# A gated mix of softmax attention and a feature-map attention on one core: one level of a sum tree changes its engine, and the last four output tiles are put together in another way

## The chip, the core and the metric

The kernel runs on one core of a Trainium2 chip. The core has five engines that work side by side: TensorE (PE in the profile, its weight loads PEld), VectorE (DVE), ScalarE (ACT), GpSimd (POOL) and SyncE (SP), which issues most DMA transfers. The metric is the device time of one execution in microseconds; before the change its median over three runs is 758.91 (758.51 to 759.47).

## The reference

`x` has 2048 tokens of 512 values. Branch A is softmax attention with 32 heads of 16 values. Branch B maps queries and keys with a small matrix per head, takes softmax of the result and of its negative, and uses these as features of a linear attention. A sigmoid gate mixes the two.

```
q, k, v = split(x @ A_wqkv)                       # 32 heads of 16
a = softmax(q k^T / 4) v  @ A_wo
q, k, v = split(x @ B_wqkv)
phi(u) = concat(softmax(u w_phi), softmax(-u w_phi))
b = (phi(q) (phi(k)^T v)) / (phi(q) sum(phi(k)) + 1e-6)  @ B_wo
g = sigmoid(sum(x * gate_w))
out = g * a + (1 - g) * b                          # 2048 x 512, bfloat16
```

## The kernel before, in words

**Units.** The scores of branch A are cut into units of 128 keys by 512 queries of one head. Four units make a pack (`p`), 16 packs a group (four heads against all keys for one chunk of 512 queries), and 32 groups the whole: 512 packs (`NPACK`), 2048 units. TensorE writes the scores of a unit to a PSUM bank (`_scores`, L1028). Most units go in pairs to ScalarE, which takes the exponential of 128x1024 values in one instruction (`_exp`, L1076). Four of the eight PSUM banks are a ring for these pairs (`NRING`); the other four are lent out in the order of the plan for everything else.

**Tiles of VectorE.** 500 units go to VectorE instead, which approximates the exponential in integer arithmetic: one instruction per unit from PSUM (L935), and for each batch of four units two further steps in SBUF (L960). `NUMS` gives how many units of each of the 32 groups go this way, and `_plan_vector` spreads them over the group's packs; `REND` (in the last group) and `REST` say how many packs at the group's end stay free. The value matmuls (L1135) add both kinds to one accumulator per group. When a group is done, VectorE transposes the accumulator (L1156), multiplies by the gate and the inverse of the denominator (L1164, L1171, L1173), and the result goes to `onTA`, in the last group by another transpose (L1187).

**Branch B.** `_b_pair` works on two token tiles of 128 at a time. It projects (L706), copies to SBUF (L1294), negates on GpSimd (L1312), takes a maximum tree on VectorE (L1315, L1317), subtracts (L1320), takes the exponential on ScalarE (L1323, 128x2048), and then sums over 16 features by a tree: the first level, 1024 sums, on VectorE (L1325), the levels of 512 and 256 (L1327) and of 128 (L1330) on GpSimd. `P_SUM` sets which levels go to GpSimd: a level of n features goes there when n is at most `P_SUM`, and the first one when `P_SUM` is over 4. An approximate reciprocal on GpSimd follows (`_reciprocal`, L1380 to L1386). There are 16 such pairs, eight for keys and eight for queries. GpSimd also masks the queries of the next two groups (L798) and multiplies in the normalisation (L1173 in all but the last two groups).

**Outputs.** Each of the 16 token tiles of the output is one PSUM bank: four matmuls with `WoB` (`_b_out`, named `outb`), four with `WoA` (in `_out`, named `outa`, all L706), then one drain to bfloat16 and one store. The last four, tiles 12 to 15, make the tail: their fourth `outa` matmul needs the very last group. Tiles 12 and 14 are drained by VectorE (L1612) and stored from SyncE's queue, tiles 13 and 15 by ScalarE (L1609) and stored from ScalarE's queue (L1614). `FIRST_OUT` and `NEXT_OUT` say how many packs before the end the first two and the last two of them may begin; `DEP_OUT` tells which of them wait only for the last VectorE tiles (`last_bits`) and which for the last value matmul (`pvs[-1]`).

**The order of the work.** A planner (`Plan.order`) holds a list of operations with costs, due times (`prio`, counted in packs) and dependences, simulates the engines and writes out a fixed order for each of them. `port` in it keeps GpSimd's work and some of VectorE's from being planned at the same time. `Plan.shift` moves every due time that is not negative by a pseudo-random amount of at most three packs; `SEEDS` has one seed for each 16 packs. Each engine then runs its list in order and waits on semaphores.

Of the kernel before, what the change touches and what calls it, by code (L numbers as in the profile page):

```python
# [7 lines left out]
ALU = mybir.AluOpType  # L8
# [3 lines left out]
D = 512  # L12
H = 32
DH = 16
TOK = 128
QCH = 512
SCALE = float(DH) ** -0.5
F32, BF16 = dt.float32, dt.bfloat16
# [47 lines left out]
class Plan:  # L66
# [43 lines left out]
    def op(self, eng, fn, cost, reads=(), writes=(), deps=(), name="", prio=0.0, rel=-99, kind="full",  # L110
           acquire=None, release=None, lat=None, array=None, strips=None, also=None):
        o = Op(eng, fn, cost, name, prio, rel, kind, self.LAT[eng] if lat is None else lat)
        found = {}
        for b in reads:
            for w in b.writers:
                found[id(w)] = w
        for b in writes:
            for w in b.readers or b.writers:
                found[id(w)] = w
            if b.readers:  # L120
                for w in b.writers:
                    found[id(w)] = w
        for d in deps:
            if d is not None:
                found[id(d)] = d
        found.pop(id(o), None)
        o.deps = list(found.values())
        for b in reads:
            b.readers.append(o)
        for b in writes:  # L130
            b.writers, b.readers = [o], []
        o.acquire, o.release, o.also = acquire, release, also
        o.strips = strips
        o.port = eng == "POOL" or eng == "DVE" and name in self.PORT
        o.held = eng == "PE" and acquire is None and name in self.HOLDING
        o.array = cost if array is None else array
        self.ops.append(o)
        return o

    SEEDS = (3340, 2114, 9789, 849, 7476, 9797, 2928, 4117, 3297, 4434, 5571, 2308, 3491, 3547, 0, 2037, 1043, 5479, 6702, 2263, 0, 95, 4494, 8165, 7230, 4451, 7158, 3400, 9901, 9455, 1584, 0, 4360, 0)  # L140

    def shift(self):
        count = {}
# [264 lines left out]
class _Kernel:  # L408
# [9 lines left out]
    URGENT, AHEAD, SOON, REST = 4, -(1 << 30), 4, 6  # L418
    QDUE, KDUE, VDUE = 20, 17, 14
    P_Q, P_MUL, P_NEG = 1, 1, 1  # L420
    P_REC, P_SUM = 0, 4
    P_BACK, RATIO, BV = 1, 1, 8
    DEN, KV2, P_MAX = 1, 0, 0
    REND = 5
    PAIRQ = 1
    P_M, P_BMUL, CHUNKS = 0, 0, 2
    GDUE = 26
# [1 line left out]
    FAST = 3  # L429
    VSOON = -2  # L430
    PADK = 2
    LAST, FIRST_OUT, NEXT_OUT, DEP_OUT = 0, 8, 0, 2
    ALONE, EARLY = 12, 10
    PVP = 10

# [442 lines left out]
                prio=100))  # L878
        self.b_gB.writers = done

    NUMS = (6, 10, 16, 14, 14, 16, 16, 19, 13, 19, 17, 12, 17, 11, 19, 19, 14, 20, 12, 16, 19, 13, 17, 16, 15, 20, 12, 20, 17, 16, 22, 13)

    def _plan_vector(self):

        NT, away = self.NT, []
        for g in range(self.NPACK // NT):
            n = self.NUMS[g]
            rest = self.REND if g == self.NPACK // NT - 1 else self.REST
            away += [4 * (NT * g + 1 + (2 * k + 1) * (NT - rest) // (2 * n)) + (len(away) + k) % 4 for k in range(n)]
        batches = [away[k:k + self.PACK] for k in range(0, len(away), self.PACK)]  # L890
        self.hooks = {}
        for k, units in enumerate(batches):
            due = max(units[0] / 4 - self.LEAD, self.VMIN)
            self.hooks.setdefault(max(0, int(due) - 4), []).append(
                lambda k=k, units=units, due=due: self._vector_batch(k, units, due))
        for n in range(1, 4 * self.NQC):
            self.hooks.setdefault(max(0, 32 * n - 30), []).insert(0, lambda n=n: self._proj_q(n))
        self.away = set(away)
# [83 lines left out]
    def _attention(self):  # L982
        plan, NT, NQC = self.plan, self.NT, self.NQC
        NU = 4 * self.NPACK
        self.exps, self.qks, self.pvs = [], [], []
        self._plan_vector()
        self.mine = [u for u in range(NU) if u not in self.away]
        self.place = {u: a for a, u in enumerate(self.mine)}
        self.late, self.opened, self.closed, self.in_group = {}, {}, {}, {}
        self.ot = {}  # L990
        self.stores = []
        self.b_outt = [Buf() for _ in range(6)]
        for b in self.b_outt[:2]:
            b.readers = list(self.b_WB.readers)
        self.b_va, self.b_vb = [Buf() for _ in range(self.NA)], [Buf() for _ in range(self.NA)]
        self.b_vs = [Buf() for _ in range(self.NST)]
        self.n_step = 0
        self.last_twin = []
        first = sum(self.GROUPS)
        assert self.mine[first - 1] < 8  # L1000
        for half in range(2):
            a = 0
            for n in self.GROUPS:
                self._qk(a, a + n, half)
                self._exp(a, a + n, half)
                a += n
        while a < len(self.mine):
            b = min(a + self.GROUPS[len(self.exps) % 2], len(self.mine))
            self._qk(a, b)
            self._exp(a, b)  # L1010
            a = b
            done = self.mine[a] if a < len(self.mine) else NU
            while len(self.pvs) < done // 4:
                self._pv(len(self.pvs))
                if len(self.pvs) in self.done:
                    self._out(self.done.index(len(self.pvs)))
# [545 lines left out]

    def _b_out(self, tt):

        job = Job()

        ops = []
        for pr in range(4):
            ops.append(self.plan.op("PE", lambda e, pr=pr: self._wide(
                e, self._bank(job), self.onTB[:, pr, tt * TOK:tt * TOK + TOK], self.WoB[:, pr, :], pr == 0, False),  # L1570
                self.c_pe(512), reads=[self.b_onTB[tt], self.b_WoB], deps=ops[-1:], name="outb",
                acquire=None if pr else job, **self._wide_kind()))
        self.outs.append((job, ops))

    def _out_tile(self, t):
        if t < self.NT - 4:
            return self.outt[:, t % 2, :]
        k = t - self.NT + 4
        return self.xT[:, k, 0:D]

    def _out(self, qc):
        op, NT, NQC = self.plan.op, self.NT, self.NQC
        for tt in range(4):
            t = 4 * qc + tt
            final = qc == NQC - 1
            due = max(self.done[qc] + 8 + 4 * tt, self._num_due(t) + 8)
            job, first = self.outs[t]
            b_onTA = self.b_onTA[qc % 3]
            if final:
                due = self.NPACK  # L1590
                deps = (self.last_bits if tt < self.DEP_OUT else [self.pvs[-1]]) + [w for b in b_onTA[:3] for w in b.writers]
            else:
                deps = [w for b in b_onTA for w in b.writers]
            for x in first:
                x.prio, x.rel = due, due - (6 if not final else self.FIRST_OUT if tt < 2 else self.NEXT_OUT)
                x.deps += deps
            if final:
                due += self.LAST
                for x in first:
                    x.prio = due  # L1600
            m = first[-1]
            for pr in range(4):
                m = op("PE", lambda e, pr=pr, qc=qc, tt=tt, job=job: self._wide(
                    e, self._bank(job), self.onTA[:, qc % 3, pr, tt * TOK:tt * TOK + TOK], self.WoA[:, pr, :], False,
                    pr == 3), self.c_pe(512), reads=[b_onTA[pr], self.b_WoA], deps=[m], name="outa",
                    prio=due + (pr == 3), **self._wide_kind())
            b_outt = self.b_outt[t % 2 if t < NT - 4 else t - NT + 6]
            if final and tt % 2:
                op("ACT", lambda e, t=t, job=job: e.activation(self._out_tile(t), self._bank(job), ACT.Copy),  # L1609
                   self.c_act(512), writes=[b_outt], deps=[m], name="out_ev", prio=due, release=job)  # L1610
            else:
                op("DVE", lambda e, t=t, job=job: e.tensor_copy(self._out_tile(t), self._bank(job)), self.c_dve(512),  # L1612
                   writes=[b_outt], deps=[m], name="out_ev", prio=due, release=job)
            s = self.dma("ACT" if final and tt % 2 else "SP", f"out{t}", lambda e, t=t: e.dma_start(  # L1614
                self.out2d[t * TOK:(t + 1) * TOK, :], self._out_tile(t)), cost=0.36, reads=[b_outt], prio=due)
            self.stores.append(s)
# [43 lines left out]
```

## Time and profile before

| What | us |
|---|---|
| median of three runs | 758.91 |
| the profiled execution | 758.1 |
| its span, first to last instruction | 756.1 |
| ScalarE busy / VectorE busy / GpSimd busy | 742.4 / 717.3 / 210.2 |
| exponentials of branch A on ScalarE (776) | 714.6 |
| end of the last exponential | 748.42 |
| end of the last projection matmul | 753.10 |
| end of the last drain | 753.82 |
| landing of the last store | 755.57 |

Rows of the profile read `line engine operation output<-input shapes xcount | busy us, mean ns of one | idle time before, by whom it ended`. In lists in order of time the first two numbers are the start and the length in us, and square brackets hold idle time and what ended it. Successive instructions of an engine overlap a little at their ends, so the step from one start to the next (0.60 us for a VectorE instruction shown with 0.69, 0.917 for an exponential shown with 1.16) is what one of them displaces. Matmul ends are modelled.

### The profile page before, as it was taken

To read this page: it belongs to the slowest core of one execution; us is meant where nothing else is said; L and a number is where in the kernel's file an instruction comes from. 1 tells how busy PE (TensorE), PEld (TensorE's weight loads), DVE (VectorE), ACT (ScalarE), POOL (GpSimd) and SP (SyncE) were. 2 spreads that over 40 slices of the span, in tenths; PEclk is the share of its full clock that TensorE was granted. 3 is DMA by queue.
4 is the path that set the end of the run, shared out by engine and by line. 5 is a ranking of instruction groups with operands and counts; after the bars stand their busy time and mean duration, and the time that the engine had idled before them with its cause. 6 is when DMAs were issued, how large, how long until landed. Compare 5 with 4: busy or idle time off the path is not lost.

```text
span 756.1 us, 17157 instructions
## 1 busy us (share of the span) xinstructions
PE 745.0 (99%) x7234; PEld 220.1 (29%) x7234; DVE 717.3 (95%) x1128; ACT 742.4 (98%) x798; POOL 210.2 (28%) x301
## 2 busy tenths in 40 slices
PE   8999999999999999999999999999999999999998
PEld 3323322322332222222222322222232223232222
DVE  5788999999999999999999999999999999999994
ACT  6999999999999999999999999999999999999996
POOL 2213205131534334134206051512324050330000
PEclk9999999999999999999999999999999999999999
DMA  9610001000001000000200212211121102111010
GB/s 216 147 25 6 9 8 15 2 3 14 2 2 15 1 8 10 6 11 3 42 15 19 54 23 34 38 27 39 16 43 29 29 22 42 24 33 26 3 15 28
DMA packets 89180, 20.78 MB, mean 27 GB/s; under 512 B 83472, under 2 KB 88592, under 8 KB 89104
## 3 DMA queue, kind: packets, MB, share of 16 engines
q1 hardware_dynamic: 87232, 18.92, 13.2%
q8 instruction: 56, 0.92, 0.5%
q10 hardware_dynamic: 1872, 0.79, 0.5%
q14 instruction: 20, 0.16, 0.1%
HBM read 4.21 MB, written 2.10 MB: 8 GB/s over the span
## 4 chain that ended last, share of the span: by engine, by line
ACT 74%; PE 17%; DVE 7%; DMA 1%; issue 0%
ACT ET L1076 71%; PE ps L1135 7%; PE ps L1028 6%; ACT bq L1323 3%; DVE vs L935 3%; PE ps L706 3%; DVE vs L960 2%; PE ps L1142 1%; DMA xT<-in_A_x_dram 1%; DVE onB L1488 0%; DVE bq L1320 0%; DVE btree L1317 0%; DVE T L1156 0%; DVE btree L1315 0%; PE ps L714 0%
## 5 line engine op out<-in xcount | busy, mean ns | idle before, releaser
L1076 ACT ACTIVATE ET<-ps 128x1024 bf16<-128x1024 f32 (+1 forms) x776 | 714.6, 1155 | 1.7 <-PE ps L1028 1.5
L935 DVE TENSOR_SCALAR vs<-ps 128x512 uint16<-128x512 f32 x500 | 322.6, 684 | 10.7 <-PE ps L1028 8.9
L1028 PE MATMUL ps<-qT,kT 32*128 32x512 bf16 (+1 forms) x2052 | 307.3, 384 | 4.7 <-ACT ET L1076 2.3
L960 DVE TENSOR_SCALAR vs<-vs 128x2048 uint16<-128x2048 uint16 (+1 forms) x250 | 240.3, 972 | 1.3 <-PE ps L1135 0.5
L1135 PE MATMUL ps<-vs,V 128*32 128x512 bf16 x2000 | 211.8, 384 | 0.9 <-DVE vs L960 0.7
L1135 PE MATMUL ps<-ET,V 128*32 128x512 bf16 x1548 | 190.4, 387 | 0.0
L1028 PEld LDWEIGHTS ps<-qT,kT 32*128 32x128 bf16 x2052 | 76.6, 91 | 298.7 <-ACT ET L1076 286.5
L1327 POOL TENSOR_TENSOR btree<-btree 128x512 f16<-128x512 f16 (+1 forms) x32 | 38.5, 1202 | 212.7 <-DVE btree L1325 211.5
L1135 PEld LDWEIGHTS ps<-ET,V 128*32 128x32 bf16 x1548 | 47.9, 94 | 77.9 <-issue 70.7
L1135 PEld LDWEIGHTS ps<-vs,V 128*32 128x32 bf16 x2000 | 48.8, 95 | 55.3 <-issue 33.3
L1142 PE MATMUL ps<-kT,zero 128*32 128x512 bf16 x604 | 61.1, 385 | 0.0
L706 PE MATMUL ps<-WB,xT 128*128 128x512 bf16 x192 | 58.6, 384 | 0.1
L1312 POOL TENSOR_SCALAR bq<-bq 128x1024 bf16<-128x1024 bf16 x16 | 19.1, 1193 | 116.9 <-DVE bq L1294 74.0
L1173 POOL TENSOR_TENSOR T<-T,rinv 128x512 bf16<-128x512 f32 x15 | 18.8, 1252 | 76.9 <-DVE rinv L1171 76.8
L798 POOL TENSOR_SCALAR qT<-qtmp,mask 128x512 bf16<-128x512 bf16 x30 | 29.9, 1001 | 33.0 <-DVE qtmp L793 32.8
L706 PE MATMUL ps<-xT,WA 128*128 128x512 bf16 x120 | 38.1, 384 | 0.1
L1323 ACT ACTIVATE bq<-bq 128x2048 bf16<-128x2048 bf16 x16 | 32.7, 2042 | 0.0
L1156 DVE STREAM_TRANSPOSE T<-ps 128x512 f32<-128x512 f32 x32 | 22.7, 709 | 9.9 <-PE ps L1135 9.9
L1294 DVE CAST bq<-ps 128x512 bf16<-128x512 f32 x32 | 21.8, 685 | 0.1
L839 POOL TENSOR_SCALAR V<-V 128x544 bf16<-128x544 bf16 x16 | 11.5, 721 | 35.8 <-DVE V L832 35.7
L706 PEld LDWEIGHTS ps<-WB,xT 128*128 128x128 bf16 x192 | 13.3, 97 | 25.1 <-issue 20.1
L706 PE MATMUL ps<-WoA,onTA 128*128 128x512 bf16 x64 | 19.8, 383 | 0.0
(89 smaller groups left out, 404.6 us busy)
## 6 DMA issues: line engine op xcount, KB each, us to landing
T<-T SPq DMA_DIRECT2D x240, 8.0 KB, 1.8
WB<-in_B_wqkv_dram SPq DMA_DIRECT2D x1, 1536.0 KB, 8.7
out_dram<-WB SPq DMA_DIRECT2D x12, 128.0 KB, 1.7
WA<-in_A_wqkv_dram SPq DMA_DIRECT2D x2, 384.0 KB, 5.1
WoB<-in_B_wo_dram SPq DMA_DIRECT2D x1, 512.0 KB, 3.9
WoA<-in_A_wo_dram SPq DMA_DIRECT2D x1, 512.0 KB, 4.9
WA<-in_A_wqkv_dram ACTq DMA_DIRECT2D x2, 128.0 KB, 3.3
WA<-in_A_wqkv_dram ACTq DMA_DIRECT2D x1, 256.0 KB, 4.6
```

Of the source, the lines that this page charges most:

```text
L706: return e.matmul(out, lhs, rhs, start=start, stop=stop)
L798: x = self.plan.op("POOL", lambda e, side=side: e.tensor_scalar(self.qT[:, s0 + side, :], tmp, self.mask[:, side:side + 1], 0.0, op0=ALU.m ...
L935: bits = lambda e, to, src: e.tensor_scalar(to, src, SCALE * LOG2E * 128.0, float(ORIGIN), op0=ALU.mult, op1=ALU.add)
L960: o = op("DVE", lambda e, k=k, src=src, dst=dst: e.tensor_scalar(dst, src, float(STEPS[k - 1]), None, op0=ALU.add), 0.16 + k * n * QCH * 0 ...
L1028: return e.matmul(out[:, cols], self.kT[32 * i:32 * i + 32, cp, kt * TOK:(kt + 1) * TOK], self.qT[32 * i:32 * i + 32, s, cols], start=True ...
L1076: o = plan.op("ACT", lambda e: e.activation(self.ET[:, a % NS:a % NS + n, cols], self.ps[:, a % NR:a % NR + n, cols], ACT.Exp, scale=SCALE ...
L1135: ins = e.matmul(self._bank(ot)[32 * i:32 * i + 32, :], v[:, v0:v0 + 32], tile, start=(kt == 0), stop=(kt == self.NT - 1), tile_position=( ...
L1142: ins = e.matmul(self._bank(ot)[32 * i:32 * i + 32, :], self.zero[:], self.kT[:, 0, 0:QCH], start=False, stop=False, tile_position=(0, 32 ...
L1156: t1 = op("DVE", lambda e: e.transpose(T1[:, side].rearrange("p b s -> p (b s)"), src()), 0.735, deps=last, writes=[b_T1[side]], name="n_t ...
L1294: [lambda e, b, k=k: e.tensor_copy(bq[:, k].rearrange("p (g s v) -> p g s v", g=8, s=2)[:, :, 0, :], b.rearrange("p (g v) -> p g v", g=8))],
L1323: op("ACT", lambda e: e.activation(flat, flat, ACT.Exp), 1.789, reads=[b], writes=[b], name="b_exp", prio=due + 1)
L1327: + [("b_sum", two(128 * n), lambda e, n=n: e.tensor_tensor(half[:, :, 0:n], half[:, :, 0:n], half[:, :, n:2 * n], ALU.add), (n <= self.P_ ...
```

## The change

It has four parts.

1. `P_SUM` goes from 4 to 8: the first level of the sum tree, 16 instructions of 128x1024, goes from VectorE to GpSimd.
2. For output tiles 12 and 14 (`_apart`) the four `outb` matmuls form a closed group of their own, due about 20 packs before the end. VectorE copies their result as float32 to a free part of `xT`. The four `outa` matmuls are then a fresh group in another bank, and VectorE's drain becomes an add of that bank and the copy.
3. Tile 15 (`RINGOUT`) takes its bank from the ring, that of the next-to-last pair of units; its matmuls wait for that pair's exponential instead of the last value matmul.
4. Constants: `FIRST_OUT` 8 to 3, `REND` 5 to 4, one tile of VectorE moved from the 16th to the 17th group and one from the 31st to the 30th, and other seeds. The number of VectorE's tiles stays 500. `CUT` and `XT` at the values given change nothing in the batches.

```diff
-    SEEDS = (3340, 2114, 9789, 849, 7476, 9797, 2928, 4117, ...)
+    SEEDS = (0, 825, 9504, 2137, 0, 1384, 1546, 5125, ...)
...
-    P_REC, P_SUM = 0, 4
+    P_REC, P_SUM = 0, 8
...
-    REND = 5
+    REND = 4
+    CUT = 4
+    XT = 0
+    XR = 2
+    RINGOUT = 1
+    APART, APART_AT = 2, 20
...
-    LAST, FIRST_OUT, NEXT_OUT, DEP_OUT = 0, 8, 0, 2
+    LAST, FIRST_OUT, NEXT_OUT, DEP_OUT = 0, 3, 0, 2
...
-    NUMS = (..., 11, 19, 19, 14, 20, ..., 17, 16, 22, 13)
+    NUMS = (..., 11, 19, 18, 15, 20, ..., 17, 17, 21, 13)
...
+    def _apart(self, t):
+        return t >= self.NT - 4 and (t - self.NT + 4) % 2 == 0 and (t - self.NT + 4) // 2 < self.APART
...
             if final:
                 due = self.NPACK
-                deps = (self.last_bits if tt < self.DEP_OUT else [self.pvs[-1]]) + [w for b in b_onTA[:3] for w in b.writers]
+                ring = tt >= 4 - self.RINGOUT
+                deps = self.exps[-2:-1] if ring else self.last_bits if tt < self.DEP_OUT else [self.pvs[-1]]
+                deps = deps + [w for b in b_onTA[:3] for w in b.writers]
...
+            if final and ring and not self._apart(t):
+                first[0].acquire = None
+            apart = self._apart(t)
+            if apart:
+                part, b_part = self.xT[:, tt, 2 * D:4 * D].bitcast(F32), Buf()
+                for x in first:
+                    x.prio, x.rel = due - self.APART_AT + 2 * tt, due - self.APART_AT - 4
+                ev = op("DVE", lambda e, job=job, part=part: e.tensor_copy(part, self._bank(job)), self.c_dve(512),
+                        writes=[b_part], deps=[first[-1]] + [r for b in self.b_xT for r in b.readers], name="outb_ev",
+                        prio=due - self.APART_AT + 2 * tt, release=job)
+                job, first = Job(), []
+            if final and ring:
+                job.bank = (self.bank2[1] + tt - 4 + self.RINGOUT) % self.NRING
...
+            elif apart:
+                op("DVE", lambda e, t=t, job=job, part=part: e.tensor_tensor(self._out_tile(t), self._bank(job), part,
+                                                                             ALU.add), self.c_dve(512), reads=[b_part],
+                   writes=[b_outt], deps=[m], name="out_ev", prio=due, release=None if ring else job)
```

## The prediction

> **What bounds the kernel now.** I read four views in this order: the busy time of each engine, the waits of ScalarE, ScalarE's instructions in order of time, and the last eleven microseconds engine by engine.
>
> Engine totals and the costliest group, from the profile's page:
> ```profile
> PE 745.0 (99%) x7234; PEld 220.1 (29%) x7234; DVE 717.3 (95%) x1128; ACT 742.4 (98%) x798; POOL 210.2 (28%) x301
> ...
> L1076 ACT ACTIVATE ET<-ps 128x1024 bf16<-128x1024 f32 (+1 forms) x776 | 714.6, 1155 | 1.7 <-PE ps L1028 1.5
> ```
> Three engines look full; the waits and ScalarE's own sequence tell which one sets the time.
> ```profile
> ACT xT L1609 <- PE ps L706: 3.6, 1, 3.6
> ...
> ACT ET L1076 <- PE ps L1028: 1.5, 3, 0.7
> ```
> ```profile
> 7.96 2.16 ACT L1076 ACTIVATE ET<-ps 128x512 bf16<-128x512 f32 x4 [0.65 <-PE ps L1028]
> 10.66 1.02 ACT L1076 ACTIVATE ET<-ps 128x1024 bf16<-128x1024 f32 x1 [0.54 <-PE ps L1028]
> 12.00 53.27 ACT L1076 ACTIVATE ET<-ps 128x1024 bf16<-128x1024 f32 x58 [0.32 <-PE ps L1028]
> ...
> 655.53 92.89 ACT L1076 ACTIVATE ET<-ps 128x1024 bf16<-128x1024 f32 x101
> ```
> From 12.00 to 748.42 us ScalarE never shows an idle gap. A full exponential adds 0.917 us: 92.89 less the 0.24 us by which the last one is drawn longer, over 101. Read one by one, the ends of successive exponentials lie 0.92 us apart nearly everywhere; only four steps are over 0.06 us longer, near 104, 354, 361 and 398 us, by 0.21, 0.09, 0.19 and 0.15, **0.63 us in all**. The change leaves the tiles that VectorE takes at 500, so it leaves ScalarE's 776 exponentials and 16 branch activations too. What can move is the head (idle gaps of 0.54 and 0.32 us once the first exponential is out), these 0.63 us, and the tail from 748.42 to 756.1.
>
> The tail on TensorE, then on VectorE:
> ```profile
> 748.27 0.62 PE L1135 MATMUL ps<-ET,V 128*32 128x512 bf16 x8
> 748.82 0.39 PE L706 MATMUL ps<-WoA,onTA 128*128 128x512 bf16 x1
> 749.05 1.03 PE L706 MATMUL ps<-WoB,WT 128*128 128x512 bf16 x4
> 749.91 0.81 PE L706 MATMUL ps<-WoA,onTA 128*128 128x512 bf16 x3
> 750.56 1.03 PE L706 MATMUL ps<-WoB,WT 128*128 128x512 bf16 x4
> 751.42 1.67 PE L706 MATMUL ps<-WoA,onTA 128*128 128x512 bf16 x7
> ```
> ```profile
> 748.94 0.72 DVE L1156 STREAM_TRANSPOSE T<-ps 128x512 f32<-128x512 f32 x1 [7.00 <-PE ps L1135]
> ...
> 750.65 0.71 DVE L1187 STREAM_TRANSPOSE onTA<-T 128x512 bf16<-128x512 bf16 x1
> 752.27 0.69 DVE L1612 CAST xT<-ps 128x512 bf16<-128x512 f32 x1 [0.91 <-PE ps L706]
> 753.13 0.69 DVE L1612 CAST xT<-ps 128x512 bf16<-128x512 f32 x1 [0.17 <-PE ps L706]
> ```
> After the last value matmul, 19 projection matmuls run 0.216 us apart. VectorE's normalisation ends at 751.36, but the matmuls that need it are mixed with three that do not, and TensorE ends at 753.10. That end releases the last cast (753.13), whose store lands at 755.57. **The tail is bound by TensorE, behind a normalisation that is ready 0.9 us before the first cast starts.**
>
> **The change, part by part.**
>
> *First sum level to GpSimd.* It takes 16 instructions off VectorE, each displacing 0.60 us (the step from one start to the next in the trace): 9.6 us of 717.3. GpSimd has no row of this size, but two neighbours:
> ```profile
> L1327 POOL TENSOR_TENSOR btree<-btree 128x512 f16<-128x512 f16 x16 | 23.7, 1481 | 211.5 <-DVE btree L1325 211.5
> L1327 POOL TENSOR_TENSOR btree<-btree 128x256 f16<-128x256 f16 x16 | 14.8, 923 | 1.2
> L1325 DVE TENSOR_TENSOR btree<-bq 128x1024 f16<-128x1024 bf16 x16 | 11.7, 729 | 1.5 <-ACT bq L1323 1.5
> ```
> Undisturbed, single instructions of these two take 1.15 and 0.67 us, so 1024 elements extrapolate to 1.15 + 0.97 = 2.12 us; the means give 1.48 + 1.12 = 2.60. The nearest one-input row (L1312, 128x1024) bounds it below at 1.04. I take 2.12: 34 us on an engine with 546 us idle. The new instruction waits for ScalarE's exponential (L1323) instead of VectorE. Behind it on GpSimd stand the rest of the tree, the reciprocal and, when due, the masks of the next queries (L798). The result comes some 1.4 us later (2.12 less 0.60 and the delay in VectorE's queue); the next half of the pair work is several units away, so I cost this at nothing. If that cover were gone, a late mask would hold score matmuls by up to those 1.4 us.
>
> VectorE's relief earns nothing directly, because ScalarE is full. At best it removes the 0.63 us of long steps. Against it, GpSimd blocks VectorE: at 114.25 the sum L1325 took 1.32 us instead of 0.69, ending 0.56 us after the GpSimd instruction that had started 0.29 us before it. Others lost 0.48 (412.84), 0.47 (659.94), 0.45 (598.31). In all, VectorE lost about 6.9 us that way, and these largest ones left no long step on ScalarE. I set relief against longer blocking: zero, with both ends (-0.63 and the rival below) kept.
>
> The Trainium skill, "SBUF — State Buffer", section "Who interferes with whom", says that a GpSimd instruction and a VectorE instruction that is in a two-port mode or has two SBUF inputs exclude each other, and the second waits for the whole of the first. The four delays above agree with it. By that rule a sum of 2.12 us can stop a VectorE step for nearly its whole length, twice what any GpSimd sum does now, which speaks against this part.
>
> *Two partial outputs.* Tiles 12 and 14 do their four second-branch matmuls about 20 packs (29 us) before the end, and VectorE copies each to SBUF: 2 x 0.60 us where it is full (14.96 of 15 us busy in 720 to 735). One tile moved from the 31st group to the 30th gives back about 1.1 us; VectorE then idles 7.00 us before 748.94, so a slip there is covered up to several microseconds, also with the last vector tiles one pack (1.4 us) later. TensorE pads its idle time with zero matmuls there (L1142), so eight more cost nothing. The final cast becomes an add with a PSUM and a float32 SBUF input; L1413, an add of that kind at 272 columns, takes 0.43 us, as does the plain copy (L1410, 0.43), so I take the same 0.69.
>
> *Ring bank for tile 15.* Its seven early matmuls need only the next-to-last exponentials instead of the last value matmul, so some can start before 748.27.
>
> *Tail sum.* From 739.6 the four tiles have 24 wide matmuls instead of 32. Thirteen ran before 748.82; with the later opening (FIRST_OUT 3 instead of 8) 6 to 13 will. That leaves 7 to 14 ahead of the four that need the normalisation; at 0.216 us from 748.82 they end at 750.3 to 751.8. So the four start at 751.42 to 751.85, instead of ending a run of seven. Now the cast starts 0.42 us after its last matmul's start; VectorE's two drains are at least 0.60 apart, so the second starts at 752.45 to 752.9, against 753.13. Its store follows as now. ScalarE's second drain starts about 752.5, against 752.55, and its store lands near 755.1 at best, so the end is 754.9 to 755.35 instead of 755.57. **Gain 0.2 to 0.7; I take 0.55.**
>
> *Seeds, tile counts, priorities.* They reorder everything without adding work. In the head the gaps of 0.54 and 0.32 may close or grow: -0.9 to +0.9, taken as zero, because the first exponentials' operands have negative due times, which seeds do not touch.
>
> Sum for the profiled execution: 758.1 (756.1 span and 2.0 around it) - 0.55 = 757.55. It lies 0.8 below the median of 758.91, so by the median **758.4**.
>
> **Rivals.**
>
> *A, slower: long GpSimd sums stop VectorE.* Place: the sixteen sums between 60 and 660 us. Of the sixteen sums of 1.15 us today, two delayed a vector step (0.23 and 0.47). With 2.12 us, about four would. Delays up to 0.6 us were absorbed, so the mechanism decides from there: a delay spread over 0.6 to 2.1 averages 1.35, 0.75 above it, and TensorE waits in order for the step, then ScalarE. 4 x 0.75 = 3.0, less 0.55: 761.3. All sixteen would be 12 us. For it: VectorE spends a third of its time in L960, which showed such delays. Against it: 6.9 us of them now cost at most 0.63. Chance 0.14.
>
> *B, faster: everything goes.* The 0.63 vanish with VectorE's new slack, the tail gives 0.7, the head 0.5: 757.1. For it: three of the four long steps lie where VectorE is the chain (340 to 398 us). Against: it needs all three together. Chance 0.14.
>
> *C, the tail does not shorten.* The final matmuls keep an order in which one tile comes last alone, or the two VectorE drains fall together at the end; then 758.9, and with small new stalls 759.5. Chance 0.24.
>
> Forecast: 0.48. A measurement of this kernel can tell about 0.2%, 1.5 us, from no change: faster is under 757.4, slower over 760.4. Forecast and C lie within: 0.72; B faster 0.14; A slower 0.14. The range reaches to B's time and part of the way to A: 757.1 to 760.6.
>
> **What would show it.** Right: exponentials still 0.917 us apart; no L1325 row on VectorE and sixteen near 2.1 us on GpSimd; fewer than 14 projection matmuls between the last value matmul and the last four; VectorE's second final drain at 752.5 to 752.9 relative to a last exponential ending at 748.4. Wrong: idle gaps on ScalarE inside 12 to 748 us, vector steps (L960) over 1.8 us beside the sums, or a last exponential that ends elsewhere than 748.4 because head or body moved.

## The result, and the profile after

The changed kernel takes 761.53 us (median of seven runs, 760.18 to 763.37) against 758.91: ratio 1.0033, 95% interval 1.0024 to 1.0042. It is **slower by 0.33%**, where 758.4 and no measurable difference were forecast. The seven runs fall into three heaps by the mean granted clock of TensorE: three of 760.2 to 760.4 at 1.000, three of 761.5 to 761.8 at 0.998, one of 763.4 at 0.995. The profiled execution is of the first kind: 760.36 us, span 758.5.

Engine totals and ScalarE's main group on the page of the changed kernel (L1076 is now L1088, L1028 is L1040):

```profile
PE 746.1 (98%) x7219; PEld 217.5 (29%) x7219; DVE 713.5 (94%) x1114; ACT 742.7 (98%) x798; POOL 242.0 (32%) x317
...
L1088 ACT ACTIVATE ET<-ps 128x1024 bf16<-128x1024 f32 (+1 forms) x776 | 714.7, 1162 | 4.2 <-PE ps L1040 4.1
...
L1337 POOL TENSOR_TENSOR btree<-bq 128x1024 f16<-128x1024 bf16 x16 | 39.7, 2483 | 175.6 <-ACT bq L1335 175.6
```

ScalarE does the same work (742.7 us busy against 742.4), the sixteen sums have moved from VectorE (713.5 against 717.3) to GpSimd (242.0 against 210.2). What differs is idle time: ScalarE's waits for score matmuls, and its instructions in order of time around 90 us:

```profile
ACT ET L1088 <- PE ps L1040: 4.1, 4, 2.0
```

```profile
84.85 1.91 ACT L1335 ACTIVATE bq<-bq 128x2048 bf16<-128x2048 bf16 x1
86.65 3.77 ACT L1088 ACTIVATE ET<-ps 128x1024 bf16<-128x1024 f32 x4
92.42 1.02 ACT L1088 ACTIVATE ET<-ps 128x1024 bf16<-128x1024 f32 x1 [2.00 <-PE ps L1040]
```

There is one new gap of 2.00 us; before, ScalarE had none from 12 us to the last exponential. I split the span at the first exponential's start and the last one's end. Before: 7.96 + 740.46 + 7.69. After: 8.03 + 742.76 + 7.74. **So 2.30 of the 2.41 us lie between the exponentials, and the tail gives nothing.** Read one by one, the steps between exponentials carry one of 2.11 us over the usual 0.917 (ending at 93.44), 0.13 and 0.24 near 705, a branch activation late by 0.23 at 190.8, and few others of 0.06 or more.

Who made the gap is seen on VectorE, GpSimd and TensorE in the same stretch of the changed kernel:

```profile
86.91 2.09 DVE L880 COPY ghB<-gh 32x16 f32<-32x16 f32 x1
89.03 1.23 DVE L971 TENSOR_SCALAR vs<-vs 128x4096 uint16<-128x4096 uint16 x1
90.17 0.68 DVE L785 CAST kT<-ps 128x512 bf16<-128x512 f32 x1
```

```profile
86.84 2.13 POOL L1337 TENSOR_TENSOR btree<-bq 128x1024 f16<-128x1024 bf16 x1 [6.02 <-ACT bq L1335]
```

```profile
88.74 0.39 PE L1040 MATMUL ps<-qT,kT 32*128 32x512 bf16 x2
90.91 0.38 PE L1040 MATMUL ps<-qT,kT 32*128 32x512 bf16 x1 [1.78 <-DVE kT L785]
```

The first of the sixteen moved sums starts at 86.84. VectorE's next instruction, a copy of 32x16 numbers that takes 0.15 to 0.17 us the other three times, is drawn from 86.91 to 89.00: it ends 0.03 after the sum. Everything in VectorE's queue behind it is late by 1.9 us, among it the cast (L785) for which TensorE's next score matmul waits (the row at 90.91); TensorE works in order, so it stands idle for 1.78 us, and ScalarE runs dry.

The tail of the changed kernel on TensorE and VectorE:

```profile
750.84 0.40 PE L1147 MATMUL ps<-ET,V 128*32 128x512 bf16 x4
751.18 1.04 PE L711 MATMUL ps<-WoA,onTA 128*128 128x512 bf16 x4
752.05 1.03 PE L711 MATMUL ps<-WoB,WT 128*128 128x512 bf16 x4
752.91 1.90 PE L711 MATMUL ps<-WoA,onTA 128*128 128x512 bf16 x7
```

```profile
753.01 0.71 DVE L1199 STREAM_TRANSPOSE onTA<-T 128x512 bf16<-128x512 bf16 x1
754.64 1.29 DVE L1647 TENSOR_TENSOR xT<-ps,xT 128x512 bf16<-128x512 f32 x2 [0.92 <-PE ps L711]
```

15 projection matmuls instead of 19 follow the last value matmul, and the last four now wait for the normalisation (it ends at 753.72, they start at 753.78). VectorE's first drain starts 3.85 us after the last exponential's end, exactly as before; its second ends at +5.14 instead of +5.40; the last store lands at +7.07 instead of +7.15.

### The profile page after: what moved, and what is told of

It is laid out like the page before. It is cut to its first block, busy times and chain, and to the rows that moved or that the text cites. A ratio compares the mean times of both kernels' runs of the same rounds, so it can differ in the third digit from the quotient of the medians.

```text
span 758.5 us, 17129 instructions
## 1 busy us (share of the span) xinstructions
PE 746.1 (98%) x7219; PEld 217.5 (29%) x7219; DVE 713.5 (94%) x1114; ACT 742.7 (98%) x798; POOL 242.0 (32%) x317
## 4 chain that ended last, share of the span: by engine, by line
ACT 73%; PE 20%; DVE 5%; DMA 1%; issue 0%; SPq 0%; DVEq 0%
ACT ET L1088 70%; PE ps L1040 7%; PE ps L1147 7%; PE ps L711 4%; ACT bq L1335 3%; DVE vs L946 2%; PE ps L827 1%; DVE vs L971 1%; DMA xT<-in_A_x_dram 1%; PE ps L1154 0%; DVE ghB L880 0%; DVE kT L785 0%; PE ps L1266 0%; DVE bq L1332 0%; DVE btree L1329 0%
## 5 line engine op out<-in xcount | busy, mean ns | idle before, releaser
L1088 ACT ACTIVATE ET<-ps 128x1024 bf16<-128x1024 f32 (+1 forms) x776 | 714.7, 1162 | 4.2 <-PE ps L1040 4.1
L1040 PE MATMUL ps<-qT,kT 32*128 32x512 bf16 (+1 forms) x2052 | 308.8, 384 | 5.5 <-DVE kT L785 1.8
L1147 PE MATMUL ps<-ET,V 128*32 128x512 bf16 x1548 | 192.9, 387 | 0.0
L1040 PEld LDWEIGHTS ps<-qT,kT 32*128 32x128 bf16 x2052 | 76.4, 91 | 305.2 <-ACT ET L1088 290.8
L1337 POOL TENSOR_TENSOR btree<-bq 128x1024 f16<-128x1024 bf16 x16 | 39.7, 2483 | 175.6 <-ACT bq L1335 175.6
L1154 PE MATMUL ps<-kT,zero 128*32 128x512 bf16 x588 | 58.9, 385 | 0.0
L1339 POOL TENSOR_TENSOR btree<-btree 128x512 f16<-128x512 f16 (+1 forms) x32 | 32.7, 1023 | 2.0
L803 POOL TENSOR_SCALAR qT<-qtmp,mask 128x512 bf16<-128x512 bf16 x30 | 22.0, 737 | 28.7 <-DVE qtmp L798 28.7
```

Of the source, the lines that this page charges most:

```text
L803: x = self.plan.op("POOL", lambda e, side=side: e.tensor_scalar(self.qT[:, s0 + side, :], tmp, self.mask[:, side:side + 1], 0.0, op0=ALU.m ...
L1040: return e.matmul(out[:, cols], self.kT[32 * i:32 * i + 32, cp, kt * TOK:(kt + 1) * TOK], self.qT[32 * i:32 * i + 32, s, cols], start=True ...
L1088: o = plan.op("ACT", lambda e: e.activation(self.ET[:, a % NS:a % NS + n, cols], self.ps[:, a % NR:a % NR + n, cols], ACT.Exp, scale=SCALE ...
L1147: ins = e.matmul(self._bank(ot)[32 * i:32 * i + 32, :], v[:, v0:v0 + 32], tile, start=(kt == 0), stop=(kt == self.NT - 1), tile_position=( ...
L1154: ins = e.matmul(self._bank(ot)[32 * i:32 * i + 32, :], self.zero[:], self.kT[:, 0, 0:QCH], start=False, stop=False, tile_position=(0, 32 ...
L1337: chain([("b_sum", two(1024), lambda e: e.tensor_tensor(half, x[:, :, 0:8], x[:, :, 8:16], ALU.add), (self.P_SUM > 4) * 2.13)] + [("b_sum" ...
```

## The experiments

The theory: **a lost race**. GpSimd started the long sum 0.07 us before VectorE came with an instruction that the planned order puts first, and held it up for the sum's whole length. A second part of it: TensorE's idle stretch of 1.78 us brings the lower clock of the slower runs. Rivals: the new order as a whole is at fault; the clock dips are unrelated.

**1. One wait added.** The first sum also waits for the VectorE step that the plan puts before it. No queue changes its order.

```diff
             p.order()
+            sums = [o for o in p.queues["POOL"] if o.name == "b_sum" and o.cost == 2.13]
+            port = [o for o in p.queues["DVE"] if o.port]
+            for o in sums[:1]:
+                o.deps.append([d for d in port if d.end <= o.start + 1e-6][-1])
```

> The changed kernel with one added wait: the first of the sixteen GpSimd sums (at 86.84 us) also waits for the VectorE step (128x4096) that the planned order puts before it; every queue keeps its order. Theory 'lost race': GpSimd started that sum 0.07 us before VectorE's next instruction, a copy of 32x16 that needs 0.16 us, and stopped it for 2.09 us; this one event makes the 2.0 us idle gap of ScalarE at 90.4. Then the gap is gone, the span goes from 758.5 to about 756.5, the granted clock is 1.000 in every run (if the half clock comes from TensorE's idle stretch) and the median falls from 761.5 to about 758.4. Rival 'order': the new order of the whole plan is at fault and the gap only shows where it gives way; then a gap of 1 us or more appears elsewhere and the span stays over 757.5. Rival 'own clock': the clock dips of 0.998 and 0.995 have nothing to do with the gap; then they stay, and the median falls by 2.0 only, to about 759.5.

Measured: 758.44 us (eleven runs, 758.1 to 759.32), ratio to the kernel before 0.9998 (0.9990 to 1.0007); no run below a clock of 0.999. VectorE, then GpSimd, of this kernel (L975 is the step, L884 the copy, L1341 the sum):

```profile
87.70 0.16 DVE L884 COPY ghB<-gh 32x16 f32<-32x16 f32 x1
87.89 1.23 DVE L975 TENSOR_SCALAR vs<-vs 128x4096 uint16<-128x4096 uint16 x1
```

```profile
89.28 2.14 POOL L1341 TENSOR_TENSOR btree<-bq 128x1024 f16<-128x1024 bf16 x1 [7.68 <-DVE vs L975]
```

The copy takes 0.16 us, the step behind it 1.23, and the sum starts 0.16 us after the step's end. The time between first and last exponential is 740.93, 1.83 less than in the changed kernel and 0.47 more than before; the profile's span is 757.5 only because its first exponential starts at 8.82. One wait takes back the loss (758.44 against 761.53), the dips of the clock are gone too, and no gap appears elsewhere; that refutes the rival of the order.

**2. TensorE's wait filled.** Eight blocks of zero matmuls stand in front of the score matmul that waits.

```diff
             p.order()
+            q = p.queues["PE"]
+            at = next(k for k, o in enumerate(q) if o.name == "vqk" and o.start > 88)
+            q[at:at] = [Op("PE", p.pad(self.ot[3]), 0.2155, "pad", 0, -99, "col", 0.2) for _ in range(8)]
```

> The changed kernel with eight more blocks of zero matmuls (0.2155 us each, adding zero to the open accumulator) in TensorE's queue in front of the score matmul that waits from 88.8 to 90.91 us. They fill TensorE's wait and free nobody. Theory 'the idle stretch lowers the clock': ScalarE's gap of 2.0 us stays and the profile's span stays 758.4 to 758.6, but all runs are at clock 1.000, so the median falls from 761.5 to about 760.3. Rival 'own clock': runs of 0.998 and 0.995 remain and the median stays near 761.5.

Measured: 760.71 (five runs, 760.48 to 762.69); the gap is still there (a step 2.11 us over the usual one), one run of five at 0.998. TensorE in that stretch (L1157 is the zero matmul):

```profile
89.28 1.91 PE L1157 MATMUL ps<-kT,zero 128*32 128x512 bf16 x32
91.13 0.39 PE L1043 MATMUL ps<-qT,kT 32*128 32x512 bf16 x1
```

The theory had a median near 760.3 and no dip. The median is 0.4 above that, and there is one dip; another run, of 761.54, has the full clock and the usual span (758.5), and its extra time of 1.2 us lies outside the span, for a reason that is not known. So it was run again with a control, below.

**3. The sums in two halves.** Each first-level sum becomes two GpSimd instructions of half the rows.

```diff
-        chain([("b_sum", two(1024), lambda e: e.tensor_tensor(half, x[:, :, 0:8], x[:, :, 8:16], ALU.add),
+        chain([("b_sum", two(1024), lambda e: [e.tensor_tensor(half[:, n:n + 16], x[:, n:n + 16, 0:8],
+                                                               x[:, n:n + 16, 8:16], ALU.add) for n in (0, 16)][-1],
```

> The changed kernel with each of the sixteen first-level sums on GpSimd as two instructions of half the rows (128x512 out each), nothing else moved. Theory 'lost race, and the length of the instruction is its price': the copy at 86.9 still arrives late, but is stopped only to the end of the first half, about 1.1 us instead of 1.9; ScalarE's gap shrinks from 2.0 to about 0.8 to 1.1 us, the span to about 757.5. Rival 'the sum as a whole must end' (the stop does not depend on the instruction's length): gap 2.0 us or more, span 758.5 to 758.8.

Measured: 761.72 (six runs), ratio 1.0045 (1.0032 to 1.0059). The gap did not shrink. VectorE and GpSimd:

```profile
87.59 1.11 DVE L880 COPY ghB<-gh 32x16 f32<-32x16 f32 x1
88.74 2.14 DVE L971 TENSOR_SCALAR vs<-vs 128x4096 uint16<-128x4096 uint16 x1
```

```profile
87.53 2.27 POOL L1337 TENSOR_TENSOR btree<-bq 128x512 f16<-128x512 bf16 x2 [6.03 <-ACT bq L1335]
```

My expectation was wrong, and shows why: the copy is indeed released after the first half (1.11 instead of 2.09). But the second half starts at 88.64, before VectorE's step comes at 88.74, and the step loses the same race again (2.14 instead of 1.22). Both delays together are the 1.9 us of the undivided sum.

This profile caught an execution at a mean clock of 0.995. Its stages before, during and after (us of the stage, busy time of each engine, granted clock, DMA):

```profile
86.00:92.50 6.50, 4.72 (x48) 1.47 (x47) 6.44 (x7) 5.10 (x5) 4.82 (x4) 1.00 0.10 20
92.50:100.00 7.50, 7.16 (x35) 1.48 (x32) 4.98 (x9) 4.97 (x5) 3.59 (x10) 0.54 0.01 2
100.00:106.00 6.00, 5.85 (x57) 1.60 (x58) 6.00 (x10) 5.66 (x8) 0.39 (x2) 1.00 0.00 0
```

The trace has the clock at one half from 92.81 to 99.64, starting 1.3 us after the end of TensorE's idle stretch (89.81 to 91.54), and ScalarE's next instructions tell the price:

```profile
93.11 1.02 ACT L1088 ACTIVATE ET<-ps 128x1024 bf16<-128x1024 f32 x1 [2.01 <-PE ps L1040]
94.90 2.11 ACT L1088 ACTIVATE ET<-ps 128x1024 bf16<-128x1024 f32 x2 [0.77 <-PE ps L1040]
97.61 1.02 ACT L1088 ACTIVATE ET<-ps 128x1024 bf16<-128x1024 f32 x1 [0.60 <-PE ps L1040]
99.12 1.02 ACT L1088 ACTIVATE ET<-ps 128x1024 bf16<-128x1024 f32 x1 [0.48 <-PE ps L1040]
```

**4. The sums back on VectorE, in the new order.** Each goes into VectorE's queue at the place that its planned start on GpSimd gives.

```diff
             p.order()
+            for o in [o for o in p.queues["POOL"] if o.name == "b_sum" and o.cost == 2.13]:
+                p.queues["POOL"].remove(o)
+                q, o.eng = p.queues["DVE"], "DVE"
+                q.insert(next(k for k, d in enumerate(q) if d.start >= o.start - 0.3), o)
```

> The changed kernel with the sixteen first-level sums taken back to VectorE, each put at the place in VectorE's queue that its planned start on GpSimd gives; all other orders stay, with the new tail. Theory 'lost race': the stop at 86.9 is gone; VectorE carries 9.6 us more and falls behind its order by 0.6 us at a time, each slip up to about 0.6 us being absorbed; span 756.2 to 757.5, clock 1.000. Rival 'the relief of VectorE is needed by this order': ScalarE idles in many places, span over 759. Rival 'order': the gap at 90.4 stays at 1 us or more.

Measured: 763.16 (five runs), ratio 1.0062 (1.0049 to 1.0075). The gap at 90 is down to 0.7, but seven idle gaps of ScalarE's exponentials lie behind the head (2.1 us; the three of the head are as before) and some 25 long steps, all along the kernel; 745.22 us between first and last exponential. My span of 756.2 to 757.5 was missed: it is 761.0. The rival that this order needs the relief came true: with the sums on GpSimd and the wait of experiment 1 the same stretch is 4.3 us shorter (745.22 less 740.93). How much of the 4.3 us is VectorE's load, and how much the places that the sums got in its queue, which the planner never weighed, this run does not separate.

**5 and 6. Control, and the filled wait again.**

> The changed kernel itself once more, as the control of the two that follow on the same chip. Every theory: 760.2 to 763.4 us, median near 761.5. 'The idle stretch lowers the clock' expects about half of the runs at a mean clock of 0.998 or less, 1.3 to 3 us slower than the rest, as in the first seven (four of seven).

> The kernel with TensorE's wait filled by zero matmuls once more, now beside the changed kernel itself. 'The idle stretch lowers the clock': clearly fewer runs at 0.998 or less than the control (one of the first five), median 0.5 to 1.3 us under the control's, and no run near 763.4. 'Own clock': the same share and the same median as the control.

Measured: the control 761.63 (six runs, 759.95 to 763.33), four of six runs at 0.998 or less. The filled wait 760.67 (eight runs, 759.96 to 761.2), none of eight. With the first runs of both: **eight of 13 against one of 13** at 0.998 or less. The control's profile has the half clock from 92.25 to 99.08. The other kernels agree: in 3 and 9, which keep the stop, four of six and five of ten runs dip; in 1, 4, 7, 8 and 10, in whose profiles no idle stretch of TensorE after the start is over 1.3 us, none of 42. So the idle stretch brings most of the dips; what the one exception came from stays open.

**7. The order of the last four matmuls.** As 1, and the last four projection matmuls serve VectorE, ScalarE, VectorE, ScalarE.

```diff
+            q = p.queues["PE"]
+            by = {o.users[0].eng: [] for o in q[-4:]}
+            for o in q[-4:]:
+                by[o.users[0].eng].append(o)
+            q[-4:] = [by[e][k] for k in range(2) for e in ("DVE", "ACT")]
```

> The changed kernel with the wait of the first experiment, and the last four projection matmuls in the order VectorE tile, ScalarE tile, VectorE tile, ScalarE tile instead of both ScalarE tiles first. Theory 'the order of the last four keeps VectorE's drains late': its first drain starts 0.43 us earlier after the last exponential (+3.4 instead of +3.85), its second ends at +4.7 to +4.8 instead of +5.14, the last store lands 0.2 to 0.4 us earlier; median 758.1 to 758.3 against 758.4 of the first experiment. Rival 'the four stores share the DMA engines': drains come earlier but the last store lands within 0.1 us of +7.07; median unchanged.

Measured: 758.32 (eleven runs), ratio to the kernel before 0.9995 (0.9986 to 1.0003). VectorE's drains, with the last exponential ending at 748.67:

```profile
752.09 1.29 DVE L1656 TENSOR_TENSOR xT<-ps,xT 128x512 bf16<-128x512 f32 x2 [0.48 <-PE ps L720]
```

They start at +3.42 and the last drain of either engine ends at +4.72, 0.42 us earlier than the last drain in 1 (+5.14). The last store lands at +7.01, only 0.06 earlier, as the rival had it: the four stores of 128 KB, now issued within 0.6 us of one another, take 1.74, 2.00, 2.01 and 2.27 us from issue to landing. In the kernel before, issued within 1.2 us, they took 1.76, 1.82, 2.04 and 1.72. What the drains gain the stores lose. What the stores wait for among themselves was not looked into.

**8. The sums on GpSimd in the old order.** The kernel before, with only the sixteen sums put into GpSimd's queue.

```diff
             p.order()
+            for o in [o for o in p.queues["DVE"] if o.name == "b_sum" and o.cost == 0.16 + 1024 * 0.000522]:
+                p.queues["DVE"].remove(o)
+                q, o.eng = p.queues["POOL"], "POOL"
+                q.insert(next(k for k, d in enumerate(q) if d.start >= o.start), o)
```

> The kernel before with one edit: its sixteen first-level sums go to GpSimd's queue at the place that VectorE's planned start gives; all other orders, the seeds and the tail stay. Theory 'lost race': with VectorE's queue not arranged around the longer instruction, several of the sixteen stop a VectorE instruction for 0.6 to 2.0 us; each stop over 0.6 us costs its excess; span 757.5 to 764 with one to six visible gaps, each of them beginning within 4 us of a sum. Rival 'the relief pays': VectorE carries 9.6 us less, the 0.63 us of long steps vanish, span 755.5 to 756.1.

Measured: 767.33 (four runs), ratio 1.0113 (1.0100 to 1.0126), all at clock 1.000. 749.34 us between first and last exponential, 8.88 more than before; ScalarE has 11 idle gaps behind the head (5.7 us). My theory had one to six gaps and a span of at most 764; it is 765.2. Seven of the sixteen sums (L1329 here) stop a VectorE step (L964) for 0.57 to 1.94 us, four of them for over 1.8. One of the four, VectorE and GpSimd:

```profile
227.83 3.16 DVE L964 TENSOR_SCALAR vs<-vs 128x4096 uint16<-128x4096 uint16 x1
```

```profile
227.78 2.13 POOL L1329 TENSOR_TENSOR btree<-bq 128x1024 f16<-128x1024 bf16 x1
```

The sum comes first by 0.05 us; the step takes 3.16 instead of 1.22. VectorE carries 9.6 us less here too, and it does not pay. Seven of the 11 gaps begin 3.5 to 6.8 us after a sum that stopped a step for 1.26 us or more. The other four begin 11 to 18 us after a sum. The chain of waits behind one of them (at 239.01) leads back to the stopped step of 227.83; behind the other three (at 128.46, 275.75 and 373.29) it runs through GpSimd itself: sum, the rest of the tree, reciprocal, then a VectorE instruction that needs it. So in this order the sum's late result has a price as well, besides the lost races.

**9. Another instruction in place of the copy.** The four small copies become reductions over an axis of length one, which give the same values.

```diff
-            done.append(op("DVE", lambda e, i=i, lo=lo, hi=hi: e.tensor_copy(
+            done.append(op("DVE", lambda e, i=i, lo=lo, hi=hi: e.tensor_reduce(
...
-                self.gh[lo:hi, 1].rearrange("p q (t i) -> p q t i", i=4)[:, :, :, i]), 0.2,
+                self.gh[lo:hi, 1].rearrange("p q (t i) -> p q t i", i=4)[:, :, :, i:i + 1], AX.X, ALU.add), 0.2,
```

> The changed kernel with its four small copies of the gate (32x16 float32, the one at 86.9 us was stopped for 1.9 us) written as a reduction over an axis of length one, which gives the same values; queues as they are. Theory 'whoever needs the shared access next is stopped': the reduction itself passes in about 0.2 us beside the GpSimd sum, but the step (128x4096) behind it is stopped until the sum ends, for 1.6 to 1.9 us; ScalarE's gap stays at 1.7 to 2.1 us, span 758.1 to 758.6 where the clock stays full. Rival 'the copy is the culprit': the step runs through at once, the gap falls under 0.5 us, span about 756.5. Rival 'every VectorE instruction is stopped': the reduction takes about 2 us like the copy.

Measured: 760.87 (ten runs, five of them at 0.998 or less), ratio 1.0029 (1.0018 to 1.0039); the step between exponentials there is 1.91 us too long. VectorE, with the sum on GpSimd from 86.64 to 88.77:

```profile
86.71 0.17 DVE L880 TENSOR_REDUCE ghB<-gh 32x16 f32<-32x16 f32 x1
86.91 2.94 DVE L971 TENSOR_SCALAR vs<-vs 128x4096 uint16<-128x4096 uint16 x1
```

The reduction passes beside the sum in 0.17 us; the step behind it is stopped instead, 2.94 for 1.22. So the copy was only the first in line that needs what the sum holds. The Trainium skill, "SBUF — State Buffer", section "Who interferes with whom", has both sides of it: a tensor reduction never contends on trn2, a tensor-scalar step in a two-port mode does, and the order of issue decides who waits; the trace agrees.

**10. The planned order kept at all sixteen sums.** As 7, with `sums` in place of `sums[:1]`.

> The seventh experiment's kernel with the planned order kept at all sixteen sums (each waits for the VectorE instruction of the shared kind that the plan puts before it) instead of the first alone. Theory 'one lost race made the loss': nothing more to gain, span 756.0 to 756.6, median 758.1 to 758.5, within 0.1% of the seventh. Rival 'the other fifteen sums cost too': the remaining long steps (0.20 near 91, 0.23 at a branch exponential, 0.14 and 0.25 near 702) shrink, median under 758.0.

Measured: 758.67 (eleven runs; I had 758.1 to 758.5), ratio 0.9999 (0.9990 to 1.0008), span 756.4, 741.00 us between first and last exponential against 740.87 in 7. GpSimd's sums now take 2133 ns in the mean instead of 2483, and nothing is gained: the other fifteen had cost nothing that such a wait takes back.

## Why the prediction was wrong

- **The bound.** Right. ScalarE's work is unchanged, and time moved only by its idle gaps and the tail. The head was rightly costed at zero: from the first exponential's start to the sixth's end it is 5.06 us in both. Where the first exponential starts differs more between executions (7.66 to 8.82 in the twelve profiles).
- **The price of the sum.** Right: 2.12 forecast, 2.13 measured undisturbed (2.48 in the mean, since VectorE stops GpSimd as well). The late result cost nothing in the new order; in the old one it did (experiment 8).
- **"I set relief against longer blocking: zero".** This step failed: the term for the longer blocking, put at nothing, was worth 1.83 us between the exponentials (742.76 against 740.93 with the one wait), and 3.1 us in the median with what it did to the clock (761.53 against 758.44). I had counted on delays up to 0.6 us being absorbed and on a mean excess of 0.75. The sums cost nothing at fifteen places, and at one a stop of 1.92 us was not absorbed at all (an idle gap on ScalarE, one of the signs I had named for being wrong). The other side, the relief, brought nothing against the kernel before: with the lost race mended, 740.93 against 740.46.
- **Rival A** had the mechanism and a chance of 0.14, but the wrong count: four stops of middling length, where there was a single one of nearly full length. One of its two precedents (0.47 us at 659.94) had been stopped by the next level of the tree, not by a sum of 1.15 us. That its 761.3 lies so near to 761.53 is luck: its 3.0 us stand against 1.83 from the stop, most of the rest of the loss came from the clock, and the 0.55 that it took off for the tail did not come. What decides is the start of each sum against the VectorE instruction planned before it, and the order of each engine is fixed: the race of 0.07 us was lost in both profiled executions of this kernel, and by as little in those of its variants that keep the order without a wait (experiments 2, 3 and 6).
- **The clock.** Missing altogether. TensorE's stop after the lost race was followed by a mean clock of 0.998 or less in eight of 13 runs, which adds about 1.4 us (0.998) or 3 us (0.995); the profile of experiment 5, with the half clock in it, has 745.42 us between first and last exponential, 2.66 more than the profile at full clock. Without it the median would be near 760.2, inside the range; with it 761.5, outside. I used the zero matmuls (L1142) only as proof of idle time on TensorE, not as a sign that its idle time has a price.
- **The tail, -0.55.** The mechanism was right on TensorE, the size off: 11 matmuls ahead of the last four, inside the 7 to 14 given; the second drain starts at +4.46, just inside +4.03 to +4.48 (my 752.45 to 752.9). So the last drain gained 0.25 us where I took 0.55, because both ScalarE tiles stand ahead of VectorE's in the last four matmuls: with VectorE's first (experiment 7) that drain starts at +4.03. And the last store lands only 0.08 us earlier; the span's tail is 7.74 instead of 7.69. The term "its store follows as now" was wrong by the other 0.17: VectorE's last two stores took 2.14 and 1.91 us instead of 1.82 and 1.72. The last three stores are now issued within 0.63 us instead of 0.86, which fits experiment 7, but that this is the cause was not shown. It is rival C's result. One of its conditions was met, too: VectorE's two drains run back to back at the end; but experiment 7 starts both 0.43 us earlier and gains only 0.06.
- The whole change without the lost race (experiment 1) comes to 758.44, my 758.4 nearly to the digit. That is luck: by the profiles the tail gave 0.6 less than forecast and the body got 0.5 longer, both to the slower side. What made up for it lies outside both: 1.8 us instead of 2.0 around the span, and perhaps the start of the first exponential, which one profile of each kernel does not settle.

## What to carry to other kernels

When an instruction moves to GpSimd, list for each of its starts the VectorE instruction just ahead of or beside it. If the plan counts on VectorE going first, a wait must enforce it, because GpSimd begins as soon as its own inputs are ready (the sum at 86.84, 0.08 us after its exponential ends); here one wait was worth 3.1 us. Splitting the GpSimd instruction does not help when its second half is queued behind the first. A stop of 1.8 us on a TensorE that is otherwise kept busy can cost its clock as well, so count what comes after the gap.

## What the runs showed of the hardware that I had not expected

- A GpSimd instruction holds up a VectorE step for its whole remaining length when it starts as little as 0.05 us earlier (2.13 us of sum, 1.94 of delay), and two of GpSimd's in a row do so twice: the waiting copy gets through between them (1.11 for 0.16), but the step behind it comes 0.10 us after the second has begun and is stopped again (2.14 for 1.22).
- An idle stretch of TensorE of 1.7 to 1.8 us, in a kernel that is busy otherwise, was followed by half clock for 6.83 us in two profiles (92.81 to 99.64 and 92.25 to 99.08), and in other executions of the same kernel the mean clock stayed at 1.000. Filling the stretch with zero matmuls left one dip in 13 runs.
- The Trainium skill, "TensorE: Matmul & The Clock Gate", section "What's actually happening", gives a half rate after an idle window of about 3.4 us and says that the window runs free of the kernel, so that its phase varies. The half rate agrees, 6.83 us is two such windows, and the free-running window fits that only some runs dip. That a whole idle window is needed does not agree as it stands: here 1.8 us were enough.
